# A drain instruction on TensorE ahead of the first scores of each chunk, in a fused attention and two-layer kernel

## The chip, the cores and the metric

The kernel runs on one core of one Trainium2 chip. The metric is the device time of one execution in microseconds (us), and the number given for a kernel is the median of its runs. A core has a matrix engine (TensorE, PE in the profile, with its weight loads shown apart as PEld), a vector engine (VectorE, DVE), an activation engine (ScalarE, ACT), GpSimd (POOL) and SyncE (SP), which issues nearly all DMAs here. Each engine works through a list of its own in order; semaphores hold an engine until another has done its part.

## The reference

There are three parts in a row, all in float32: attention of 12288 queries over 768 pooled keys, then two feed-forward layers with 2048 hidden units.

```python
kv_pool = kv.reshape(B, H // 4, 4, W // 4, 4, C).mean(axis=(2, 4))   # 768 keys of 128
k = v = kv_pool.reshape(B, -1, C) @ w_sr
s = (q @ k.T) / sqrt(C);  a = softmax(s)                              # q: 12288 x 128
x = a @ v
h = x @ w_in1;  x = elu(h) @ w_out1                                   # 128 -> 2048 -> 128
h = x @ w_in2;  out = leaky_relu(h, 0.01) @ w_out2
```

## The kernel before

The queries are cut into 24 chunks of 512 (`NCH`, `CH`), and a chunk into four tiles of 128 queries (`NJ`). Each float32 operand of a product is kept as a high and a low part, and a product is three matmuls (`mm3`, lines 87 to 89): high by high, low by high, high by low.

For each tile, `scores` puts six matmuls of 384 columns into PSUM (two halves `b` of the 768 keys, three matmuls each), VectorE takes the row maximum, ScalarE the exponential, GpSimd scales by the inverse of the sum. The exponentials are then turned: for the first two chunks on TensorE (`NEARLY = 2`, `turn_early`, line 419), for the others by a store to DRAM and a load, and a transpose on VectorE (`send`, `fetch`, `turn`). `values` (line 439) makes the attention output of a chunk with 18 matmuls, in two steps. Then each of the two layers has eight units for a chunk (`NU`): `up` is six matmuls of 512 columns, `down` six more. Between them stand the activation and the split into high and low parts: for the first layer ScalarE (`relu`, line 474, and `elu_exp`), VectorE (`elu`, line 481) and GpSimd (`elu_head`), for the second layer ScalarE alone, and for both VectorE's `tail` (line 501). The second layer runs ten units behind the first (`D2`).

The order on each engine is set by a planner at the end of the function: each piece of work is a `step` with an engine, an assumed length, the steps it comes after, and a due time. The planner simulates the engines with these lengths and calls the function of each step in the order that comes out, so the program is written in that order. The scores of a chunk are due 24 units (`AHEAD`) ahead of the first unit that uses them, so from the fourth chunk on they stand among the `up` and `down` matmuls of earlier chunks. The accumulators of scores, values, `up` and the weight preparation share three PSUM places.

PE's list around the first scores of a chunk in the middle of the program is this (the names are output tile, weight and moving operand; `x2h` and `x2l` are the second layer's input, `kt_hi`, `kt_lo` the keys, `qh`, `ql` the queries; in brackets the semaphores that a matmul waits for, by the engine that raises them).

```order
L89 MATMUL ps<-x2h,wl_i_3_86 128x512
L87 MATMUL ps<-x2h,wh_i_3_85 128x512
L88 MATMUL ps<-x2l,wh_i_3_85 128x512
L89 MATMUL ps<-x2h,wl_i_3_86 128x512
L87 MATMUL ps<-kt_hi,qh 128x384 [waits PE_49,Activation_49]
L88 MATMUL ps<-kt_lo,qh 128x384
L89 MATMUL ps<-kt_hi,ql 128x384
```

The first scores wait for two semaphores, PE's own (the previous use of that PSUM place, 24 matmuls back) and ScalarE's. The first of the two is waited for by an instruction of its own, an EVENT_SEMAPHORE, which stands in the list just ahead of the matmul.

Of the kernel before, what the change touches and what calls it, by code (L numbers as in the profile page):

```python
# [24 lines left out]
NEARLY = 2  # L25
# [14 lines left out]
def pooled_attention_elu_leaky_kernel(  # L40
# [20 lines left out]
    nc = tc.nc  # L61
# [24 lines left out]
    def mm3(ps, w_hi, w_lo, x_hi, x_lo, start, stop):  # L86
        nc.tensor.matmul(ps, w_hi, x_hi, start=start, stop=False)  # L87
        nc.tensor.matmul(ps, w_hi, x_lo, start=False, stop=False)  # L88
        nc.tensor.matmul(ps, w_lo, x_hi, start=False, stop=stop)  # L89
# [254 lines left out]
    def scores(t, b):  # L344
        c, j = divmod(t, NJ)
        hi, lo = (x[:, j * P:(j + 1) * P] for x in qT[c])
        ps = sc_t[t]
        ks = slice(b * HK, (b + 1) * HK)
        mm3(ps[:, b, :HK], hi, lo, kt_hi[:, ks], kt_lo[:, ks], True, True)

# [246 lines left out]
    for c in range(NCH):  # L597
# [5 lines left out]
        for j in range(NJ):  # L603
# [3 lines left out]
            if j >= 2:  # L607
                after.append(av_done.get(c - 1))
            s0 = step(PE, 0.52, lambda t=t: scores(t, 0), after, key)
            s1 = step(PE, 0.52, lambda t=t: scores(t, 1), [s0], key)  # L610
            take(s0, "ps", None, 3, lambda ps, t=t: sc_t.__setitem__(t, ps))
            last_sc = s1
# [228 lines left out]
```

## Time and profile before

| | us |
|---|---|
| median of 3 runs | 1349.71 |
| lowest and highest of them | 1345.48 and 1368.37 |
| the profiled execution, its own time | 1346.46 |
| its span, first to last instruction | 1344.5 |
| PE busy within the span | 1307.3 |
| DVE, ACT, POOL busy | 1106.1, 994.2, 377.0 |

The profiled execution's time is 2.0 us longer than its span; that is what lies around the program. Busy time of an engine is the time in which at least one of its instructions runs; PE's matmuls overlap in the profile, so the time that a matmul takes in a row of them is read from one start to the next, not from its length.

### The profile page before, as it was taken

The page shows a single profiled execution, that of the slowest core. Times are in us where ns is not written, and L with a number is a line of the kernel's source. Part 1 is how long each engine was busy: PE and PEld are TensorE (multiplying, and loading weights), DVE is VectorE, ACT ScalarE, POOL GpSimd, SP SyncE. Part 2 cuts the span into 40 slices and gives each one's busy share as a digit, 9 for nine tenths or more (in the row PEclk, how much of TensorE's full clock was granted, in tenths as well). Part 3 has the DMA queues.
Part 4 walks back from the last instruction along what each step waited for, and adds up shares of the span by engine and source line. Part 5 has one row for each costly group of instructions (what it writes and reads, how often), then busy time and mean ns, then how long its engine had stood idle before and what let it go on. Part 6 is the DMA issues. An engine that isn't in the chain of part 4 may idle for free.

```text
span 1344.5 us, 16194 instructions
## 1 busy us (share of the span) xinstructions
PE 1307.3 (97%) x5800; PEld 1077.7 (80%) x5800; DVE 1106.1 (82%) x1271; ACT 994.2 (74%) x1197; POOL 377.0 (28%) x310
## 2 busy tenths in 40 slices
PE   5788999999999999999999999999999999999998
PEld 5566788888888888888888888888888888888886
DVE  6899887887887988978878878879789788788664
ACT  2667887787777787877877877777877778778675
POOL 0334332323232322323323232233233233232110
PEclk8999999999999999999999999999999999999999
DMA  8243322322223223223223122232232232222001
GB/s 244 55 140 97 93 61 73 86 56 79 68 55 88 65 55 87 72 61 87 55 79 86 53 81 67 55 88 66 55 87 69 65 87 55 71 79 55 0 8 16
DMA packets 169375, 97.58 MB, mean 73 GB/s; under 512 B 104656, under 2 KB 153936, under 8 KB 169296
## 3 DMA queue, kind: packets, MB, share of 16 engines
q1 hardware_dynamic: 168096, 96.36, 26.4%
q8 instruction: 46, 0.75, 0.2%
q10 hardware_dynamic: 1200, 0.20, 0.1%
q14 instruction: 33, 0.27, 0.1%
HBM read 55.64 MB, written 40.89 MB: 72 GB/s over the span
## 4 chain that ended last, share of the span: by engine, by line
PE 92%; DVE 4%; ACT 1%; issue 1%; DMA 1%; SPq 0%; POOL 0%; DVEq 0%; POOLq 0%
PE ps L88 15%; PE ps L87 15%; PE ps L89 15%; PE py L88 13%; PE py L87 13%; PE py L89 13%; PE ps L439 7%; DVE gl L501 1%; PE ps L238 1%; DMA kv<-in_kv_dram 1%; DVE g L481 1%; DVE a L213 1%; DVE a L206 0%; DVE nm L353 0%; ACT e L360 0%
## 5 line engine op out<-in xcount | busy, mean ns | idle before, releaser
L501 DVE TENSOR_TENSOR gl<-g,gh 128x1024 fp32r<-128x1024 f32 x384 | 470.2, 1248 | 76.9 <-POOL gh L487 61.3
L487 POOL TENSOR_SCALAR gh<-g 128x1024 fp32r<-128x1024 f32 x192 | 216.1, 1126 | 674.5 <-DVE g L481 654.1
L88 PE MATMUL py<-gl,wh_o 128*128 128x512 f32 x768 | 303.5, 395 | 2.7 <-DVE gl L501 2.7
L474 ACT ACTIVATE r<-ps 128x1024 f32<-128x1024 f32 x192 | 197.2, 1027 | 142.2 <-PE ps L89 141.8
L87 PE MATMUL py<-gh,wh_o 128*128 128x512 f32 x768 | 300.8, 392 | 0.0
L89 PE MATMUL py<-gh,wl_o 128*128 128x512 f32 x768 | 299.6, 390 | 0.0
L481 DVE SCALAR_TENSOR_TENSOR g<-r,ps 128x1024 f32<-128x1024 f32 x192 | 233.5, 1217 | 70.7 <-ACT r L477 67.3
L493 ACT ACTIVATE gh<-ps 128x1024 fp32r<-128x1024 f32 x192 | 197.2, 1027 | 56.9 <-PE ps L89 55.2
L477 ACT ACTIVATE r<-r 128x1024 f32<-128x1024 f32 x192 | 203.6, 1061 | 4.7
L497 ACT ACTIVATE g<-ps 128x1024 f32<-128x1024 f32 x192 | 196.5, 1023 | 0.0
L379 POOL TENSOR_SCALAR e<-e,rs 128x768 f32<-128x768 f32 x88 | 136.9, 1556 | 173.6 <-DVE rs L369 160.6
L88 PEld LDWEIGHTS py<-gl,wh_o 128*128 128x128 f32 x768 | 144.4, 188 | 31.8 <-DVE gl L501 5.1
L89 PEld LDWEIGHTS py<-gh,wl_o 128*128 128x128 f32 x768 | 144.3, 188 | 31.6
L87 PEld LDWEIGHTS py<-gh,wh_o 128*128 128x128 f32 x768 | 144.2, 188 | 29.9
L87 PE MATMUL ps<-x2h,wh_i 128*128 128x512 f32 x384 | 150.5, 392 | 1.8 <-DVE g L481 1.8
L87 PE MATMUL ps<-xh,wh_i 128*128 128x512 f32 x384 | 151.0, 393 | 0.3
L88 PE MATMUL ps<-x2l,wh_i 128*128 128x512 f32 x384 | 151.2, 394 | 0.0
L88 PE MATMUL ps<-xl,wh_i 128*128 128x512 f32 x384 | 151.2, 394 | 0.0
L89 PE MATMUL ps<-xh,wl_i 128*128 128x512 f32 x384 | 149.4, 389 | 0.0
L89 PE MATMUL ps<-x2h,wl_i 128*128 128x512 f32 x384 | 149.4, 389 | 0.0
L428 DVE TENSOR_TENSOR el<-e,eh 128x768 fp32r<-128x768 f32 x88 | 100.0, 1137 | 19.5 <-ACT eh L424 19.4
L360 ACT ACTIVATE e<-ps,nm 128x768 f32<-128x768 f32 x96 | 85.9, 895 | 36.1 <-DVE nm L353 33.8
(80 smaller groups left out, 1582.2 us busy)
## 6 DMA issues: line engine op xcount, KB each, us to landing
d<-e SPq DMA_DIRECT2D x88, 384.0 KB, 2.6
x<-d SPq DMA_DIRECT2D x88, 384.0 KB, 3.1
qn<-in_q_dram SPq DMA_DIRECT2D x96, 64.0 KB, 3.5
kv<-in_kv_dram SPq DMA_DIRECT2D x12, 512.0 KB, 8.5
out_dram<-y SPq DMA_DIRECT2D x94, 64.0 KB, 2.4
ws<-in_moe_w_in_dram SPq DMA_DIRECT2D x8, 512.0 KB, 3.9
ws<-in_moe_w_out_dram SPq DMA_DIRECT2D x8, 512.0 KB, 3.9
out_dram<-y ACTq DMA_DIRECT2D x2, 64.0 KB, 2.9
```

The lines of the kernel that those rows point to most:

```text
L87: nc.tensor.matmul(ps, w_hi, x_hi, start=start, stop=False)
L88: nc.tensor.matmul(ps, w_hi, x_lo, start=False, stop=False)
L89: nc.tensor.matmul(ps, w_lo, x_hi, start=False, stop=stop)
L379: nc.gpsimd.tensor_scalar(out=x, in0=e, scalar1=rs_t.pop(t), scalar2=1.0, op0=ALU.mult, op1=ALU.mult)
L428: nc.vector.tensor_tensor(out=lo, in0=e_t.pop(t), in1=f(hi), op=ALU.subtract)
L474: nc.scalar.activation(out=r_u[n], in_=ps_u[n], func=AF.Relu, scale=-1.0)
L477: nc.scalar.activation(out=r_u[n], in_=r_u[n], func=AF.Exp, scale=-1.0)
L481: nc.vector.scalar_tensor_tensor(out=g_u[n], in0=r_u.pop(n), scalar=-1.0, in1=ps_u.pop(n), op0=ALU.add, op1=ALU.max)
L487: nc.gpsimd.tensor_scalar(out=gh_u[n], in0=g_u[n], scalar1=1.0, scalar2=0.0, op0=ALU.mult, op1=ALU.add)
L493: nc.scalar.activation(out=gh_u[n], in_=ps_u[n], func=AF.Prelu, alpha=0.01)
L497: nc.scalar.activation(out=g_u[n], in_=ps_u.pop(n), func=AF.Prelu, alpha=0.01)
L501: nc.vector.tensor_tensor(out=gl_u[n], in0=g_u.pop(n), in1=f(gh_u[n]), op=ALU.subtract)
```

## The change

In `scores`, ahead of the first half (`b == 0`) of the first tile (`j == 0`) of each chunk from the third on (`c >= NEARLY`), a drain instruction is given to TensorE. It reads and writes no tile and has no semaphore of its own. It is no step of the planner, so the order of all other instructions on all five engines stays as it was, and so do their waits. There are 22 such drains, one for each of the chunks 2 to 23 (counted from 0); the one of each chunk stands between the last matmul ahead and the EVENT_SEMAPHORE of the first scores, where the chunk has one.

```diff
@@ def scores(t, b):
         c, j = divmod(t, NJ)
         hi, lo = (x[:, j * P:(j + 1) * P] for x in qT[c])
         ps = sc_t[t]
+        if b == 0 and j == 0 and c >= NEARLY:
+            nc.tensor.drain()
         ks = slice(b * HK, (b + 1) * HK)
         mm3(ps[:, b, :HK], hi, lo, kt_hi[:, ks], kt_lo[:, ks], True, True)
```

## Rows read from the trace of the kernel before

**Rows 1.** Page: busy time, granted clock in 40 slices, chain that ended last

```profile
PE 1307.3 (97%) x5800; PEld 1077.7 (80%) x5800; DVE 1106.1 (82%) x1271; ACT 994.2 (74%) x1197; POOL 377.0 (28%) x310
...
PEclk8999999999999999999999999999999999999999
...
PE 92%; DVE 4%; ACT 1%; issue 1%; DMA 1%; SPq 0%; POOL 0%; DVEq 0%; POOLq 0%
```

**Rows 2.** Windows: stretch, its length, busy us (count) by engine, clock, DMA

```profile
0.00:64.00 64.00, 41.65 (x199) 33.24 (x199) 44.38 (x90) 29.04 (x61) 12.12 (x19) 0.95 0.54 157
64.00:122.00 58.00, 51.61 (x201) 36.69 (x202) 53.51 (x69) 40.66 (x58) 23.22 (x22) 0.97 0.40 118
122.00:169.00 47.00, 44.02 (x185) 33.67 (x183) 42.93 (x55) 35.64 (x46) 15.87 (x13) 1.00 0.32 90
...
189.30:1183.50 994.20, 994.20 (x4447) 829.41 (x4446) 837.83 (x932) 759.80 (x894) 288.45 (x228) 1.00 0.27 71
```

**Rows 3.** Line 87 on PE from 189 to 1190 us: the scores' first matmuls

```profile
L87 PE MATMUL ps<-kt_hi,qh x154: 335/338/338, 189.3 to 1184.0; 128*128 128x384 f32 x154
```

**Rows 4.** Timeline (start, length), PE: the first scores of chunk 12

```profile
607.38 0.39 PE L88 MATMUL ps<-x2l,wh_i 128*128 128x512 f32 x1
607.61 0.39 PE L89 MATMUL ps<-x2h,wl_i 128*128 128x512 f32 x1
607.84 0.34 PE L87 MATMUL ps<-kt_hi,qh 128*128 128x384 f32 x1
608.01 0.34 PE L88 MATMUL ps<-kt_lo,qh 128*128 128x384 f32 x1
```

**Rows 5.** Timeline: PE's last matmul and VectorE's first step after it

```profile
1338.61 0.39 PE L89 MATMUL py<-gh,wl_o 128*128 128x512 f32 x1
1339.04 0.72 DVE L526 STREAM_TRANSPOSE y<-py 128x512 f32<-128x512 f32 x1 [2.29 <-PE py L89]
```

**Rows 6.** Line 836, program's end: PE's drains (ns min/median/max, first and last start)

```profile
L836 PEldq DRAIN  x2: 13/1128/2242, 1336.8 to 1344.1; - x2
```

**Rows 7.** Line 825, program's start: PE's and POOL's drains

```profile
L825 POOLq DRAIN  x1: 187/187/187, 0.3 to 0.3; - x1
...
L825 PEldq DRAIN  x1: 8/8/8, 0.3 to 0.3; - x1
```

**Rows 8.** Line 87: PE's sequencer instructions that wait for a semaphore

```profile
L87 PEldq EVENT_SEMAPHORE  x233: 51/51/51, 28.3 to 1327.9; - x117
```

**Rows 9.** Timeline, PE: two starts after an idle stretch, chunk 2's scores first

```profile
62.95 0.40 PE L240 MATMUL ps<-b,plus 128*128 128x512 f32 x1
63.96 0.44 PE L87 MATMUL ps<-kt_hi,qh 128*128 128x384 f32 x1 [0.61 <-DVE g L481]
64.23 0.34 PE L88 MATMUL ps<-kt_lo,qh 128*128 128x384 f32 x1
...
132.96 0.50 PE L87 MATMUL ps<-x2h,wh_i 128*128 128x512 f32 x1 [1.82 <-DVE g L481]
133.30 0.39 PE L88 MATMUL ps<-x2l,wh_i 128*128 128x512 f32 x1
```

**Rows 10.** Timeline, PE: chunk 3's first scores and the next wait

```profile
121.90 0.34 PE L87 MATMUL ps<-kt_hi,qh 128*128 128x384 f32 x1
...
126.94 0.50 PE L88 MATMUL py<-gl,wh_o 128*128 128x512 f32 x1 [0.92 <-DVE gl L501]
```

**Rows 11.** Timeline: a start of PE that no semaphore of the profile explains

```profile
38.62 0.63 PE L419 MATMUL ps<-ident,x 128*128 128x128 f32 x4 [1.83 <-issue]
```

**Rows 12.** PE's longest wait from 64 to 122 us (total, times, longest)

```profile
PE ps L238 <- ACT e L360: 3.0, 1, 3.0
```

## Prediction

> **What bounds the kernel now.** I read the page first, then stretches of the span, then single matmuls. The page says that PE is busy 97% of the span at full granted clock but for the first slice, and that 92% of the chain that ended last is PE [rows 1]. An average says nothing of where a bubble would land, so the stretches come next. From 189.3 to 1183.5 us PE is busy 994.20 of 994.20 us: no idle nanosecond in a thousand microseconds, while VectorE has 156 us and ScalarE 234 us to spare [rows 2]. Only ahead of that is PE idle: 22 us up to 64, 6 us up to 122, 3 us up to 169 [rows 2]. So there are two kinds of place for a drain. Where PE waits for others anyway, a bubble of PE can vanish in the next wait. Where PE never waits, each nanosecond that PE loses moves all that follows, and the end with it, because no engine has a later wait on PE's path to give it back.
>
> Which drains fall where? In the long stretch the scores' first matmul (line 87) stands 154 times, from 189.3 to 1184.0 [rows 3]; a chunk has eight of these (four tiles, two halves), so this is 19 whole chunks, 4 to 22, and the first two matmuls of chunk 23. That makes 20 drains in the saturated stretch. The other two are chunk 2's at 63.96 [rows 9] and chunk 3's at 121.90 [rows 10].
>
> **What one drain costs, step by step.** Without it, the matmul ahead of the first scores of chunk 12 starts at 607.61 and the scores at 607.84 [rows 4]: 0.23 us from start to start, although the earlier matmul's row is 0.39 long. The rows of neighbouring matmuls overlap by 0.16; the weights of the scores are loaded in that time too. A drain that holds the list until PE is empty takes this overlap away. The trace has one drain behind work, at the program's end: it begins at 1336.8, lasts 2.242 us and so ends at 1339.04 [rows 6], and PE's last matmul had started at 1338.61 [rows 5]. VectorE, which waits for that matmul, starts at 1339.04 as well. So PE is empty 0.43 us after the start of its last matmul, and the drain does wait for it.
>
> The restart then has three pieces. The EVENT_SEMAPHORE ahead of the scores can no longer run early; such instructions take 51 ns [rows 8]. From there to the first weight load and matmul the grouped rows have no price; I put 0.05 us, an estimate that takes it to be another sequencer instruction of that kind. Last, the first matmul after an idle stretch holds up the second: at 63.96 and 64.23 the scores' first two starts are 0.27 apart where rows 4 have 0.17, and at 132.96 and 133.30 two matmuls of 512 columns are 0.34 apart instead of 0.23 [rows 4, 9]. That is 0.10 more for the scores. The sum for one drain: 0.43 + 0.05 + 0.05 + 0.10 - 0.23 = 0.40 us.
>
> The lower bound is the lost overlap alone, 0.39 - 0.23 = 0.16 us, were the restart free. For the upper bound I add the longest that a drain with nothing to wait for takes anywhere at the program's start, 0.187 us on POOL, PE's own being 0.008 [rows 7]: 0.40 + 0.19 = 0.59 us. I take 0.40, since its largest pieces are PE's own rows and PE's own drains on an empty engine are 8 and 13 ns [rows 6, 7]. Nothing speaks for a gain in the saturated stretch, since there is no wait of PE that an earlier emptying could shorten.
>
> What the drain does to the others: while it holds PE's list, the matmuls already handed to PE go on, so only the bubble at its end is felt. Behind it stand the scores themselves and then a `down` and an `up` of other chunks; ScalarE, VectorE and GpSimd get their inputs 0.40 us later and have slack of more than a tenth of the stretch [rows 2]. No DMA hangs on it: the queries of the chunk were loaded and split before.
>
> The Trainium skill has two places on this. "TensorE: Matmul & The Clock Gate", section "Part 2: What happens when you issue a matmul", says that the tail of one matmul lies under the start of the next and that a lone matmul at the full clock takes (398 + N) / 2.4 ns, a weight load P / 1.2. An estimate by that page: a drain lays open 398 / 2.4 = 166 ns of tail and 107 ns of weight load, 0.27 us a drain, 5.5 us for 20. The trace agrees on the first (0.16 of overlap) and is near on the second (0.10); what the sequencer does after a drain is in neither figure, so I stay with 0.40.
>
> **The sum.** Saturated stretch: 20 x 0.40 = 8.0 us (bounds 20 x 0.16 = 3.2 and 20 x 0.59 = 11.8). Chunk 2: PE has just been idle 0.61 us there, waiting for VectorE's `elu`, and pays the restart already [rows 9]; what covers the drain is that wait, so 0, and 0.05 if the drain is handled after it. Chunk 3: five microseconds later PE waits 0.92 for VectorE's `tail`, and at 132.96 it waits 1.82 for VectorE's `elu` [rows 9, 10]; VectorE is the busier engine there, 42.93 of 47 us against 44.02 of overlapping PE rows [rows 2], so I put 0, with 0.4 if those waits move along with PE.
>
> Against the profiled execution's own 1346.46 (its span of 1344.5 and 2.0 around it) this makes 1354.5. That execution was 3.3 us faster than the median of the runs, 1349.71, which would give 1357.7. Between the two I say **1356**. A difference under 2%, 27 us, is about what a measurement of this kernel cannot tell from no change; the forecast is well inside.
>
> **Rivals.** *The drain passes at once.* If on PE it only runs through the sequencer and does not hold the matmuls behind it, each costs some 10 ns (8 and 13 on an empty engine [rows 6, 7]) in a list that runs ahead of PE, and the time stays at 1346.5 to 1349.7. Against it stands the 2.242 us of the drain at the end [rows 6], which fits PE's last matmul to within the rows' rounding. The Trainium skill bears on this from both sides: "Perfetto Trace Analysis", section "Per-instruction lifecycle", counts a drain among the instructions of the sequencer alone, and "PSUM — Partial Sum Buffer", section "Engine vs sequencer instructions", says that the sequencer waits for earlier work only to be dispatched, but that a drain waits for the engine to be idle. By the trace the second holds. 8%.
>
> *The lost lead costs more than the bubble.* The end's drain began 2.2 us before PE was empty [rows 6], so PE's sequencer runs at least that far ahead of the matmuls. Each drain throws the lead away, and the instructions behind it have to be handed over afresh. If that were slow, PE would start late with no semaphore to blame, as once at 38.62, where 1.83 us passed so [rows 11]. Then 20 x 1.83 = 37 us: 1383 from the profiled execution's time, 1386 from the median, slower by over 2%. It decides once a drain costs over 27 / 20 = 1.35 us. For it speaks only that one row; against it that after the idle stretches of rows 9 only the second matmul comes late, and by 0.10. 5%.
>
> *The clock falls.* Mean granted clocks of 0.95 and 0.97 stand in the first two stretches, in the second with a wait of PE of 3.0 us [rows 2, 12]. 0.97 over 58 us is 1.7 us lost; if every drain brought that, 20 x 1.7 = 35 us, 1381. But the stretch from 122 to 169 has waits of 0.92 and 1.82 us and shows 1.00 [rows 2, 9, 10], and a drain leaves PE empty for well under 0.3. 2%.
>
> **How the numbers follow.** The forecast has 84%, the three rivals 8, 5 and 2, and 1 is left for a gain over 2%, for which I know no mechanism. The range has the forecast's bounds from either base: 1346.5 + 3.2 is 1349.7, and 1349.7 + 11.8 is 1361.5. I give 1349 to 1362; that also holds part of the first rival, and leaves the two slow ones out. Within 2% are the forecast and the first rival, 92%; slower the two others, 7%; faster 1%.
>
> **What would show it.** In the profile after: 22 more drains of PE, under the line of the new call, each some microseconds long; ahead of the scores of chunks 4 to 23 a start-to-start distance of some 0.53 us where 0.23 stands, then 0.27 instead of 0.17, and all else the same; the period of a chunk longer by 0.40; PE idle by about 0.1 to 0.2 us for each drain in the stretch that now has none. Starts that stay 0.23 apart would show the first rival; distances over 1.5 us, or several matmuls in a row late, the second; a granted clock under 1.00 in the long stretch, the third. The step most open is the 0.05 between the drain's end and the first weight load, for which no row stands.

## The result, and the profile after

The changed kernel took 1357.26 us in the median of 4 runs (1356.18 to 1358.9), the kernel before 1348.96 in 4 runs. One of these four, 1368.37, is a slow execution, which the ratio leaves out. The ratio is 1.0063, with a 95% interval of 1.0049 to 1.0078: some 8.5 us slower, well under the 2% that count as a change, but clear of no change. The prediction had held that a difference of this size could not be told from none; these runs tell it. The forecast was 1356, with 1349 to 1362.

First the windows of the kernel after (stretch, length, then busy us and count of PE, PEld, DVE, ACT and POOL, clock, DMA share, GB/s), to be laid beside [rows 2]:

```profile
0.00:64.00 64.00, 42.86 (x194) 35.70 (x194) 42.78 (x86) 25.95 (x56) 10.34 (x16) 0.89 0.50 150
...
189.30:1183.50 994.20, 989.90 (x4413) 820.55 (x4412) 828.49 (x926) 752.74 (x885) 287.25 (x227) 1.00 0.26 71
```

The stretch that had no idle time now has 4.30 us of it, at a granted clock of 1.00, the upper of TensorE's two levels (2.4 GHz). The waits of PE say where (who waited for whom: us in total, times, longest), and line 349, the new call, what stands there:

```profile
PE ps L87 <- PE ps L89: 4.5, 20, 0.3
```

```profile
L349 PEldq DRAIN  x22: 1450/4310/4310, 64.7 to 1191.4; - x22
```

Twenty waits of PE for itself, each for the matmul ahead of a chunk's first scores: the twenty drains of the saturated stretch, some 0.22 us each. A drain lasts 4.31 us, since PE's sequencer reaches it that long before PE has done the matmuls already handed over. Now the timeline on PE (start, length, idle time before in brackets) at the first scores of chunks 4, 12 and 23, and at those of chunks 2 and 3, the answers to [rows 4, 9, 10]. In the names of these rows, as in the list that was shown for the kernel before, the moving operand stands first and the weight second (`kt_hi` moves, `qh` is the weight).

```profile
66.94 0.44 PE L87 MATMUL ps<-kt_hi,qh 128*128 128x384 f32 x1 [0.61 <-DVE g L483]
...
125.85 0.40 PE L89 MATMUL py<-gh,wl_o 128*128 128x512 f32 x1
126.33 0.44 PE L87 MATMUL ps<-kt_hi,qh 128*128 128x384 f32 x1
...
131.11 0.50 PE L88 MATMUL py<-gl,wh_o 128*128 128x512 f32 x1 [0.78 <-DVE gl L503]
...
193.88 0.42 PE L87 MATMUL ps<-kt_hi,qh 128*128 128x384 f32 x1 [0.22 <-PE ps L89]
...
615.12 0.40 PE L89 MATMUL ps<-x2h,wl_i 128*128 128x512 f32 x1
615.73 0.41 PE L87 MATMUL ps<-kt_hi,qh 128*128 128x384 f32 x1 [0.22 <-PE ps L89]
615.99 0.34 PE L88 MATMUL ps<-kt_lo,qh 128*128 128x384 f32 x1
...
1195.90 0.41 PE L87 MATMUL ps<-kt_hi,qh 128*128 128x384 f32 x1 [0.22 <-PE ps L89]
```

At chunk 12 the scores start 0.61 us after the matmul ahead instead of 0.23, and the second start is 0.26 later instead of 0.17 [rows 4]. At chunk 2 nothing is new: the idle time of 0.61 us is the same as in [rows 9]. At chunk 3 the scores start 0.48 us after the matmul ahead instead of 0.23, so the drain does open a gap; but PE's next wait, for VectorE's `tail`, shrinks from 0.92 [rows 10] to 0.78 us, and the matmul that waits starts 5.26 us after the last one ahead of the scores, where the kernel before takes 5.27. So the gap is gone by the end of that wait.

The first scores of chunks 4 and 23 in the kernel before:

```profile
189.34 0.34 PE L87 MATMUL ps<-kt_hi,qh 128*128 128x384 f32 x1
...
1183.50 0.34 PE L87 MATMUL ps<-kt_hi,qh 128*128 128x384 f32 x1
```

From chunk 4's first scores to chunk 23's it takes 1195.90 - 193.88 = 1002.02 us instead of 994.16. That is 7.86 us for the 19 drains of chunks 5 to 23, 0.41 each; chunk 4's makes it 8.3. The spans of the two profiled executions differ by more, 1356.9 - 1344.5 = 12.4 us. The rest lies ahead of chunk 4: its scores start at 193.88 instead of 189.34, and chunk 2's, where the first drain stands, already 3.0 us late, with a mean granted clock of 0.89 up to 64 us instead of 0.95 [rows 2]: in both executions TensorE, idle for over 20 us of that stretch, was granted the lower level (1.2 GHz) for a part of it, and for a longer part in that of the changed kernel. The experiments show that this belongs to the execution and not to the drains.

### The profile page after: what moved, and what is told of

It reads as the page before. It is cut to its first block, busy times and chain, and to the rows that moved or that the text cites. A ratio compares the mean times of both kernels' runs of the same rounds, so it can differ in the third digit from the quotient of the medians.

```text
span 1356.9 us, 16216 instructions
## 1 busy us (share of the span) xinstructions
PE 1315.1 (97%) x5800; PEld 1079.1 (80%) x5800; DVE 1103.5 (81%) x1271; ACT 993.6 (73%) x1197; POOL 375.7 (28%) x310
## 4 chain that ended last, share of the span: by engine, by line
PE 92%; DVE 4%; issue 1%; ACT 1%; DMA 1%; SPq 0%; POOL 0%; DVEq 0%; POOLq 0%
PE ps L87 15%; PE ps L89 15%; PE ps L88 15%; PE py L89 13%; PE py L88 13%; PE py L87 12%; PE ps L441 7%; PE ps L238 1%; DVE gl L503 1%; DMA kv<-in_kv_dram 1%; DVE g L483 1%; DVE a L213 0%; PE ps L421 0%; DVE a L206 0%; DVE nm L355 0%
## 5 line engine op out<-in xcount | busy, mean ns | idle before, releaser
L89 PE MATMUL py<-gh,wl_o 128*128 128x512 f32 x768 | 303.0, 394 | 0.0
```

## The experiments

All times are of single profiled executions unless an interval stands with them; "chunk 4 to 23" is the time from the first scores of the one to those of the other, 994.16 us in the kernel before and 1002.02 in the changed one.

**Only the two drains at the start.**

```diff
-        if b == 0 and j == 0 and c >= NEARLY:
+        if b == 0 and j == 0 and c in (2, 3):
```

> Drains ahead of the first scores of chunks 2 and 3 alone. Bubble theory (a drain costs only where PE never waits): no change that can be measured, ratio 0.998 to 1.003 to the kernel before, at most 0.4 us from chunk 3; the distance from chunk 4 to chunk 23 stays at the 994.16 us of the kernel before. Rival (the two drains at the start cause the 1.6 us that the changed kernel lost between the first scores of chunks 2 and 4): 1 to 2 us slower, and the same loss between these chunks. Second rival (the offset of 3 us that stands before the first drain belongs to the change as well): 3 to 4.5 us slower.

Measured: ratio 0.9982 to the kernel before, interval 0.9951 to 1.0013, so no change. From its timeline on PE:

```profile
193.48 0.34 PE L87 MATMUL ps<-kt_hi,qh 128*128 128x384 f32 x1
```

Chunk 4 to 23 is 994.19 (193.48 to 1187.67). Chunk 4 begins at 193.48, late as in the changed kernel, although the time is that of the kernel before; other executions below that have no drain ahead of chunk 4 begin it at 193.12 and 193.36, and two with drains there at 189.86 and 190.31. So executions differ by some 4 us in their start, whatever the drains, and the profiled one of the kernel before had the short start. The start goes with the granted clock: its mean up to 64 us is 0.95 where chunk 4 begins at 189.34 (the kernel before) and 189.86, 0.92 at 190.31, and 0.89 in the seven executions that begin it at 193.06 to 193.88. Why the clock differs from execution to execution was not tried.

The second rival, 3 us or more, falls by the interval. The interval alone would still allow the first, 1 to 2 us between the first scores of chunks 2 and 4; but there it takes 126.31 us with the two drains, and 126.28 and 126.42 in two executions below that have no drain there and the same mean clock (0.89 up to 64 us, 0.97 from 64 to 189). So that rival falls too, and the two drains at the start cost nothing that these runs can show.

**One drain.**

```diff
-        if b == 0 and j == 0 and c >= NEARLY:
+        if b == 0 and j == 0 and c == 12:
```

> One drain, ahead of the first scores of chunk 12. Bubble theory: the start of these scores comes 0.61 to 0.62 us after the matmul ahead (0.227 without), the next start 0.25 after that (0.177 without), 0.46 us in all, and nothing else changes. Theory of the give-back A (a drain leaves PE in the closer rhythm, 173 to 174 ns a scores matmul instead of 177, which the kernel before has up to chunk 6 and then loses): chunks 12 to 15 at least take about 52.27 us instead of 52.33, and some of the 0.46 is gone by chunk 16. Theory of the give-back B (it comes from the drains that follow, or from less traffic): chunk 13 begins 0.40 to 0.46 late and every later chunk just as late, with scores at 177 ns again.

```profile
611.11 0.39 PE L89 MATMUL ps<-x2h,wl_i 128*128 128x512 f32 x1
611.72 0.41 PE L87 MATMUL ps<-kt_hi,qh 128*128 128x384 f32 x1 [0.22 <-PE ps L89]
611.97 0.33 PE L88 MATMUL ps<-kt_lo,qh 128*128 128x384 f32 x1
```

The timeline shows the whole price at one place: 0.61 and 0.25 where 0.23 and 0.17 stand without a drain, 0.46 us. The stretch from chunk 4 to 23 was 993.68 us (193.12 to 1186.80) all the same, half a microsecond under the kernel before: this execution kept the closer of two rhythms of its scores from chunk 4 to 10 and from 12 to 20. So the rhythm was there before any drain, and came back with this one; one drain could not settle whether it was the cause.

**Between the two halves of the first tile.**

```diff
-        if b == 0 and j == 0 and c >= NEARLY:
+        if b == 1 and j == 0 and c >= NEARLY:
```

> The drain of each chunk from the third on stands between the two halves of the first tile's scores, where no semaphore is waited for and a matmul has 384 columns on both sides. Bubble theory: PE empty 0.385 us after the start of the last matmul (0.34 of row and 0.045), the next start 0.06 after that, so 0.445 from start to start instead of 0.176, and the second matmul 0.08 late: 0.35 us a drain instead of 0.465, before what is given back; the whole 1352 to 1354. Lost-lead theory (the cost is in handing the list over again after the drain): as much as in the changed kernel, 0.39 and 0.075 a drain, since the lead is lost as well.

```profile
611.70 0.34 PE L89 MATMUL ps<-kt_hi,ql 128*128 128x384 f32 x1
612.12 0.44 PE L87 MATMUL ps<-kt_hi,qh 128*128 128x384 f32 x1
612.40 0.34 PE L88 MATMUL ps<-kt_lo,qh 128*128 128x384 f32 x1
```

On the timeline 0.42 from start to start and 0.28 to the next, so 0.25 + 0.10 = 0.35 us a drain, as the bubble theory had it, against 0.46 ahead of the tile. The execution took 1353.42, with a short start (chunk 4 at 190.31); chunk 4 to 23 is 999.97, 5.8 us over the kernel before or 0.31 for each of the 19 drains in between, the 0.35 less some 0.05 that the closer rhythm gives back.

The 0.61 and the 0.42 part at the drain's end. By the drain's row PE is empty 0.36 us after the start of its last matmul here, and the next matmul starts 0.06 after that; ahead of the tile, in the changed kernel, it is 0.44 and 0.17. The first difference is that of the rows' lengths (384 against 512 columns) but for some 0.03. The second goes with the EVENT_SEMAPHORE: in all the runs shown here, a drain that has no such instruction, no second drain and no wait for another engine behind it is followed by a matmul after 0.06 us (75 times), and one with it after 0.17 us or more. At chunk 3's scores, which have none, the same matmul behind 512 columns starts after 0.48 us and not 0.61. So an instruction that is free while the list runs ahead costs some 0.11 us behind a drain. No run adds or removes it alone.

**Two drains in a row.**

```diff
         if b == 0 and j == 0 and c >= NEARLY:
             nc.tensor.drain()
+            nc.tensor.drain()
```

> Two drains in a row ahead of the first scores of each chunk from the third on. Bubble theory: the second finds PE empty and takes about 0.01 us with at most 0.07 until the list goes on, so 0.63 to 0.70 us from the matmul ahead to the scores instead of 0.617, 0 to 1.6 us more in all than the changed kernel. Rival (a drain has a price of its own whatever is in flight): another 0.39 a drain, 8 us more.

The second drain's line, and the timeline on PE:

```profile
L350 PEldq DRAIN  x22: 13/13/13, 66.7 to 1196.4; - x22
```

```profile
614.82 0.40 PE L89 MATMUL ps<-x2h,wl_i 128*128 128x512 f32 x1
615.50 0.42 PE L87 MATMUL ps<-kt_hi,qh 128*128 128x384 f32 x1 [0.29 <-PE ps L89]
```

The second takes 13 ns and moves the start from 0.61 to 0.68: 0.07 us, and 1003.54 from chunk 4 to 23 (193.06 to 1196.60), 1.5 over the changed kernel. A drain by itself costs no more than that; the first one pays for what is in flight.

**All four tiles.**

```diff
-        if b == 0 and j == 0 and c >= NEARLY:
+        if b == 0 and c >= NEARLY:
```

> A drain ahead of the first scores of each of the four tiles of a chunk, from the third chunk on: 88 instead of 22, 80 of them where PE never waits. Bubble theory without give-back limits: 80 times the net 0.40 is 32 us, 1378 to 1382. Bubble theory with the give-back as a limited thing (0.065 a chunk, once a chunk): 20 x 0.40 and 60 x 0.465, 36 us, 1382 to 1386, ratio 1.026 to 1.028. Rival (a bubble is partly hidden by slack that PE has somewhere in a chunk): well under 24 us. Rival (lost lead adds up when drains come closer together): over 45 us.

Measured: 1385.49 us in the median of 4 runs, ratio 1.0268 (1.0246 to 1.029), within the second sum of the expectation. A drain ahead of another tile opens the same gap, here that of the third tile of chunk 12, 0.62 us from start to start:

```profile
655.09 0.40 PE L89 MATMUL ps<-x2h,wl_i 128*128 128x512 f32 x1
655.71 0.42 PE L87 MATMUL ps<-kt_hi,qh 128*128 128x384 f32 x1 [0.22 <-PE ps L89]
```

Chunk 4 to 23 is 1028.66 us (193.59 to 1222.25), 26.64 over the changed kernel for 57 more drains: 0.467 each. Nothing in a chunk of the saturated stretch absorbs a bubble, and bubbles do not grow when they come closer.

**Ahead of both halves.**

```diff
-        if b == 0 and j == 0 and c >= NEARLY:
+        if j == 0 and c >= NEARLY:
```

> A drain ahead of both halves of the first tile's scores of each chunk from the third on; the second comes three matmuls after the first, before PE's list can run ahead again. Bubble theory: the second costs as much as the drain between the halves alone, 0.35 us, so 0.465 and 0.35 a chunk less what is given back, some 0.75: 15 us over the kernel before. Lost-lead theory: the second, with hardly any lead to lose, costs clearly less than the first, under 0.15, and the sum stays under 0.60 a chunk.

```profile
L349 PEldq DRAIN  x44: 610/1135/4310, 61.9 to 1198.4; - x44
```

```profile
614.89 0.34 PE L89 MATMUL ps<-kt_hi,ql 128*128 128x384 f32 x1
615.31 0.43 PE L87 MATMUL ps<-kt_hi,qh 128*128 128x384 f32 x1
615.58 0.34 PE L88 MATMUL ps<-kt_lo,qh 128*128 128x384 f32 x1
```

The drains of line 349 now last from 0.61 us: those between the halves, 0.77 us long at chunk 12, are reached shortly before PE is empty, so there is little lead to lose. In the kernel that has them alone they last some 3.1 us. They still take 0.42 and 0.27 from start to start, as there. From chunk 4 (189.86) to 23 (1198.34) it is 1008.48, or 0.75 more a chunk, the number expected. But for the 0.11 of the EVENT_SEMAPHORE, lost lead is not what is paid for.

**Drains at three chunks.**

```diff
-        if b == 0 and j == 0 and c >= NEARLY:
+        if b == 0 and j == 0 and c in (8, 14, 20):
```

> Drains ahead of the first scores of chunks 8, 14 and 20 alone. Theory of the give-back A (PE's matmuls have two rhythms, with 0.869 us from the first to the sixth scores matmul or with 0.884; a long run without a gap slips from the first to the second, and a drain sets the first again): whatever the rhythm ahead of a drain, 0.869 in the tiles behind it, for some chunks at least; each drain costs 0.39 and 0.07 at its place, and a chunk behind it takes 52.26 to 52.28 us instead of 52.33 until the rhythm slips again; chunk 4 to chunk 23 994.0 to 994.9 us against 994.16 of the kernel before. Theory B (the rhythm is one of the whole execution and has nothing to do with drains): at least one of the three drains that meets the second rhythm leaves it as it was.

The first and the sixth scores matmul of the third tile of chunk 7, ahead of a drain, and of chunk 8, behind one, on the timeline:

```profile
378.44 0.34 PE L87 MATMUL ps<-kt_hi,qh 128*128 128x384 f32 x1
...
379.32 0.33 PE L89 MATMUL ps<-kt_hi,ql 128*128 128x384 f32 x1
...
431.21 0.34 PE L87 MATMUL ps<-kt_hi,qh 128*128 128x384 f32 x1
...
432.08 0.34 PE L89 MATMUL ps<-kt_hi,ql 128*128 128x384 f32 x1
```

0.88 ahead and 0.87 behind, and the same at the other two places: two chunks ahead of each drain the scores had slipped into the wider rhythm, and behind each they were back in the closer one, for four chunks behind the first two and to chunk 23 behind the last. Two chunks behind the drain take 559.81 - 455.27 = 104.54 us, where the kernel before takes 104.66 from 450.84 to 555.50:

```profile
455.27 0.34 PE L87 MATMUL ps<-kt_hi,qh 128*128 128x384 f32 x1
...
559.81 0.34 PE L87 MATMUL ps<-kt_hi,qh 128*128 128x384 f32 x1
```

```profile
450.84 0.34 PE L87 MATMUL ps<-kt_hi,qh 128*128 128x384 f32 x1
...
555.50 0.34 PE L87 MATMUL ps<-kt_hi,qh 128*128 128x384 f32 x1
```

Chunk 4 (193.36) to 23 (1188.15) is 994.79, within what theory A gave. Theory B falls: all three drains met the wider rhythm, and none left it.

**At another place.** No drain in `scores`; instead, in `up`:

```diff
         m, c, u = units[n]
+        if i == 0 and m == 1 and u == 0 and c >= NEARLY:
+            nc.tensor.drain()
         wh, wl = wblk(f"i{m}", 2 * u + i)
```

> The drains stand at another place: ahead of the first layer's first up matmul of each chunk from the third on, 22 as well, all where PE never waits, with 512 columns on both sides and a wait for VectorE but no EVENT_SEMAPHORE ahead of the matmul. Bubble theory, with the pieces as measured: 0.444 us from the start of the matmul ahead to the drain's end, 0.06 to the next start, so 0.50 instead of 0.23, and the second matmul 0.11 late: 0.385 a drain, 8.5 us for 22 less what the rhythm gives back (0.02 to 0.07 a chunk), 7 to 8.5 in all. Rival (the cost is bound to the scores, their accumulator or their waits): another sum than that by 0.1 a drain or more, or a cost at the scores still.

```profile
593.39 0.39 PE L89 MATMUL py<-gh,wl_o 128*128 128x512 f32 x1
593.86 0.49 PE L87 MATMUL ps<-xh,wh_i 128*128 128x512 f32 x1
594.20 0.40 PE L88 MATMUL ps<-xl,wh_i 128*128 128x512 f32 x1
```

0.47 and 0.34 instead of 0.23 and 0.23: 0.24 + 0.11 = 0.35 us a drain, a little under the 0.385 expected, at a place that has nothing to do with the scores. Chunk 4 (193.75) to 23 (1195.22) is 1001.47, 7.3 us over the kernel before. Some 0.5 of it stand ahead of the first of the 19 drains in between, at 224.68, where matmuls of 512 columns followed one another by 0.233 us instead of 0.229; the drains account for the other 6.8, or 0.36 each. Here the scores stay mostly in the wider rhythm: a drain at this place does not close it as those at the scores do.

## Why the prediction was right

The mechanism is the one forecast. *Saturated stretch:* no slack takes up a bubble; one drain, twenty and eighty cost 0.45 to 0.47 us each at their place. *Start:* chunks 2 and 3 at nothing, the second because the wait behind it shrinks, as said. *The drain holds the list:* 4.31 us long with matmuls in flight, 13 ns with none. The first rival, a drain that passes at once, is out. The second, the lost lead, is out as well: the drains between the halves, with little lead, cost what they cost with much, and none comes near the 1.83 us of that rival. The third is out too: the granted clock stayed at 1.00 in the saturated stretch.

The size is right by two errors that cancel, and the sum of 0.40 did not foresee that: this much of the hit is luck.

- *The restart was too small.* I had put 0.53 us from start to start; it is 0.61, and PE is idle 0.22 us a drain, not 0.1 to 0.2. The 0.43 until PE is empty nearly holds (0.44), and so do the 51 ns of the EVENT_SEMAPHORE as a row. The 0.05 that I put for what no row showed is about 0.12 in this place: 0.06 stand behind a drain without the EVENT_SEMAPHORE too, and the rest comes with it.
- *The second matmul was nearly right:* 0.26 instead of 0.17, so 0.08 to 0.09 late, not 0.10. One drain costs 0.46 us at its place.
- *A give-back was missing.* The kernel before runs its scores in the wider rhythm from chunk 6 on, and a drain just ahead of the scores closes it; that returns some 0.07 us a chunk, so that the net is 0.41. The drains added in the other three tiles have nothing to give back and cost 0.467 each. The first and the sixth scores matmul of the third tile of chunk 12, in the kernel before and in the changed one, are 0.89 and 0.87 apart:

```profile
636.06 0.34 PE L87 MATMUL ps<-kt_hi,qh 128*128 128x384 f32 x1
...
636.95 0.33 PE L89 MATMUL ps<-kt_hi,ql 128*128 128x384 f32 x1
```

```profile
644.01 0.34 PE L87 MATMUL ps<-kt_hi,qh 128*128 128x384 f32 x1
...
644.88 0.34 PE L89 MATMUL ps<-kt_hi,ql 128*128 128x384 f32 x1
```

- *The base.* The profiled execution before had a start some 4 us shorter than most. The sum against its own time, 1354.5, lay below all four runs after; the sum against the median, 1357.7, hit the 1357.26. At an equal mean granted clock over the whole execution the two kernels are some 8 us apart, as the sum of 8.0 has it: 1358.17 and 1358.90 at 0.992 against 1349.98 to 1350.80 for the kernel before in the runs beside the experiments, and 1356.34 at 0.994 against 1347.84 to 1348.60.

The Trainium skill's page "TensorE: Matmul & The Clock Gate", section "Part 2: What happens when you issue a matmul", gave the estimate of 0.27 us a drain, from the tail and the weight load. The pieces nearest to these two measure 0.21 us (the 0.44 until PE is empty, less 0.23) and 0.08 (the second matmul). The 0.17 from the drain's end to the next matmul, which the estimate leaves out, is over a third of the 0.46.

The Trainium skill's page "PSUM — Partial Sum Buffer", section "Engine vs sequencer instructions", says that a drain waits for the engine to be idle. The drains of 4.31 us behind a full list and of 13 ns on an empty engine agree.

## What to carry to other kernels

Price a drain between matmuls as the overlap of two neighbouring matmuls, plus the restart (the instructions that stand between it and the next matmul, which are free only while the sequencer runs ahead), plus the second matmul that comes late: here 0.35 us without an EVENT_SEMAPHORE behind it and 0.46 with one. Multiply by the places where the engine never waits, and by those alone. A profiled execution is a base with a scatter of its own: before a few microseconds are put down to an edit, see whether they stand ahead of the first place that it touches, and whether the granted clock was the same there.

## What the runs showed that I had not expected

PE's sequencer is 4.31 us ahead of its matmuls at the scores, but the program's last drain showed only 2.24 [rows 6]. The matmuls of the scores have two rhythms, 0.87 or 0.88 us over six starts, that hold for chunks at a time; the whole is 0.07 us a chunk, or 0.13%. A run slips into the wider one at chunks that differ (6 or 11 without a drain ahead of them, four chunks after two of the three drains, nine after the single one), and a drain just ahead of the scores brings the closer one back: it did so in all four places where a lone drain met the wider one, while the kernel before kept the wider one from chunk 7 to 23. What makes it slip was not tried and stays open.
